# The opening of a fused convolution and max-out kernel: block 0's products put together, and work handed between engines

## The chip, the cores and the metric

The kernel runs on one core of a Trainium2 chip. A core has a matrix engine (TensorE, PE in the profile, with its weight loads as PEld), three engines that work element by element (VectorE or DVE, ScalarE or ACT, GpSimd or POOL) and a sequencer that issues the DMA transfers here (SyncE or SP). Each engine runs its own instructions in the order in which the program gives them, and waits on semaphores for the others. The metric is the device time of one execution, in microseconds (us).

## The reference: what is computed

```
w   = softmax(weight, axis=-1)                    # 8 heads x 7 taps
y   = causal convolution of x along the sequence  # x: 8 x 4160 x 192, 24 channels a head
      y[b, s, h, :] = sum_k w[h, k] * x[b, s + k - 6, h, :]
h   = max(y @ w1, y @ w2, y @ w3)                 # 33280 tokens, 192 -> 768
out = h @ w_out                                   # 768 -> 192
```

Inputs and output are float32.

## The kernel before, in words

The 33280 tokens are cut into 65 blocks of 512. The kernel uses max(a, b, c) = c + max(0, a - c, b - c). It forms the differences w1 - w3 and w2 - w3 once (`wd`, made by `make_wd`), computes max(0, y(w1 - w3), y(w2 - w3)) with one relu on ScalarE and one maximum on VectorE (`top`, L500 and L501), and adds y(w3 w_out) through a 192x192 matrix `m16` that it also makes once (`make_m`). The 768 columns of the weights are handled as 6 tiles of 128, and the opening speaks of thirds: tiles 0 to 1, 2 to 3 and 4 to 5.

All work runs in the order in which the program is written (the schedule is manual), so the order of the lines is the order on each engine.

Weights. `load_wa` brings channels 0 to 127 and `load_wb` channels 128 to 191 of w1, w2 and w3, in pieces of columns, all through the SP queue. For the last 64 channels, w1 lies in partitions 0 to 63 and w2 in 64 to 127 of one slot, so w3's 64 rows are needed in both halves: `copy_w3` (L314 to L316) copies them from the lower to the upper half. `make_wd(n, j0, j1)` (L312) subtracts for n = 0 (w1, channels 0 to 127), n = 1 (w2, the same channels) and n = 2 (channels 128 to 191 of both). `cast_w3` makes a 16-bit copy of w3, `cross_wd` (L323) swaps halves of `wd`.

The band. The convolution is done on TensorE as a product with a banded matrix of the softmax weights. L293 makes the band's 38 distinct columns for all heads by small matmuls into PSUM, in two tiles cut at column `CUT`; L297 copies them to the four diagonal places of `band`, the first tile on ScalarE, the second on VectorE. `keep_warm` (L261) issues matmuls on zeros.

Blocks 0 to 3 are "dense". `load_x` brings their rows as float32 (`xf`); `cast_dense` (L216) writes them as 16-bit into two zeroed arrays `xz[t][0]` and `xz[t][1]`, by slots of 32 channels; blocks 0 and 2 share one pair of arrays, 1 and 3 the other. `conv_dense` (L388) multiplies them with the band: its half n = 0 gives channels 0 to 127, its half n = 1 channels 128 to 191 in both halves of the partitions. Each half is 40 matmuls into its own PSUM tile `D`, copied (L393) by the engine that the call names to `yd[:, 0]` or `yd[:, 2]`. `cross` (L399) writes `yd[:, 1]`, the swapped halves of `yd[:, 0]`, for the blocks that need it (2 and 3). Later blocks have rows laid out differently; part of their `xf` (partitions 32 to 63) must be zeroed first (`zero_x`, L137 and L140) before `load_x` may bring them.

Products of blocks 0 and 1 (`l1_dense`, L536) are named by letters: F is the product over channels 0 to 127, H the one over channels 128 to 191, where both sides (w1 and w2) use half of TensorE's rows each and run side by side. The tiles named `lp` and `lq` live in the PSUM pools p and q, `lw` in pool w. For blocks 0 and 1 `l1_dense` and `tops` alternate, two tiles of 128 columns at a time. Block 0 runs F then H, block 1 H then F.

The opening, as written before (lines L687 to L712): differences of the first third on VectorE, conv of block 0 (copies on ScalarE and VectorE), loads of blocks 4 to 6, the casts of block 1, F of block 0's first two tiles, w3's later columns copied by GpSimd and most of the later differences there, conv of block 1 (half n = 1 first, copied by ScalarE; then n = 0, copied by VectorE), H of block 0's first two tiles, and then block 1's first two tiles, H then F.

Of the kernel before, what the change touches and what calls it, by code (L numbers as in the profile page):

```python
# [11 lines left out]
FP16 = mybir.dt.float16  # L12
# [3 lines left out]
P = 128  # L16
# [12 lines left out]
def kernel(  # L29
# [177 lines left out]
    def cast_dense(t, copies, slots_=range(CYC // 32)):  # L207
        xf, _, parts = xin.pop(t)
        for v, copy in enumerate(copies):
            if copy is None:  # L210
                continue
            for s in slots_:
                cut = GRP * (32 * s // GRP + 1)
                a, b = (32 * s, cut) if v == 0 else (cut, 32 * s + 32)
                for (rl, q0, q1) in parts:
                    copy(  # L216
                        out=xz[t][v][0:rl, q0:q1, :].rearrange("p q (k c) -> p q k c", c=CYC)[:, :, :, a:b],
                        in_=xf[0:rl, q0:q1, :].rearrange("p q (k c) -> p q k c", c=CYC)[:, :, :, a:b])
# [33 lines left out]
    make_identity(nc, ident[:])  # L252
    ident16 = const.tile([P, P], FP16)
    nc.gpsimd.tensor_copy(out=ident16[:], in_=ident[:])
    idle = const.tile([P, NBLK], FP16)
    nc.vector.memset(idle[:], 0.0)
    def keep_warm(n, pool=psw, tag="w"):

        ps = pool.tile([P, NBLK], FP32, tag=tag, name="idle")
        for _ in range(n):  # L260
            nc.tensor.matmul(ps[:], lhsT=idle[:, 0:P], rhs=idle[:], start=True, stop=True)  # L261

    line = const.tile([NHEAD, LINE // 2], FP16, name="line")[:, 0:WIN + 31]
    nc.vector.memset(line[:], 0.0)
    for v in range(2):
        nc.vector.memset(xz[0][v][:], 0.0)  # L270
# [5 lines left out]
    bands = const.tile([P, LINE // 2 * ceil(NHEAD * BAND_W * 2 / LINE)], FP16, name="band")  # L276
    band = bands[:, 0:NHEAD * BAND_W].rearrange("p (h w) -> p h w", w=BAND_W)
    nc.vector.memset(band[:], 0.0)
    keep_warm(5, psp, "p")
    wrec = const.tile([NHEAD, SMALL], FP32, name="wrec")[:, 0:1]  # L280
    nc.vector.reduce_sum(out=wrec[:], in_=wexp[:], axis=AXX)
    nc.vector.reciprocal(out=wrec[:], in_=wrec[:])
    zero_x(4)
    nc.vector.tensor_scalar_mul(out=line[:, 31:31 + KW], in0=wexp[:, 0:KW], scalar1=wrec[:])
    for v in range(2):
        nc.vector.memset(xz[1][v][:], 0.0)  # L286
    cast_dense(0, (nc.vector.tensor_copy, nc.vector.tensor_copy))
    CUT = 28
    for lo, hi, copy in ((0, CUT, nc.scalar.copy), (CUT, WIN, nc.vector.tensor_copy)):
        bps = psq.tile([32, hi - lo + 3, NHEAD], FP32, tag="q", name=f"band_{lo}")  # L290
        for c in range(lo, hi):

            nc.tensor.matmul(bps[:, c - lo:c - lo + 4, :].rearrange("p c h -> p (c h)"),  # L293
                             lhsT=line[:, WIN - 1 - c:WIN + 31 - c],
                             rhs=ident16[0:NHEAD, 0:4 * NHEAD], start=True, stop=True)
        for a in range(4):
            copy(out=band[32 * a:32 * a + 32, :, 32 * a + lo:32 * a + hi],  # L297
                 in_=bps[:, 0:hi - lo, :].rearrange("p c h -> p h c"))
    zero_x(5)
    keep_warm(3, psp, "p")  # L300

# [12 lines left out]
    def copy_w3(copy, j0, j1):  # L314
        f = slice(P * j0, P * j1)
        copy(out=w3s[HALF:P, 1, f], in_=w3s[0:HALF, 1, f])  # L316
# [59 lines left out]
    def conv_dense(t, copies, pools=((None, None),) * 2, order=(0, 1)):  # L376


        yd = dense[t] = ydp.tile([P, NC, NBLK], FP16, tag="yd", name=f"yd_{t}")
        for n in order:  # L380
            slots_ = ((0, 1, 2, 3), (4, 5, 4, 5))[n]
            pool, tag = pools[n]
            ps = (pool or psw).tile([P, NBLK], FP32, tag=tag or "w", name=f"D{n}_{t}")
            for (q, b, row_lo, rlen, lo, hi, cc) in chunks_of[t]:
                for v in range(2):
                    for g, s in enumerate(slots_):
                        h = (32 * s + 31 * v) // GRP
                        nc.tensor.matmul(  # L388
                            ps[32 * g:32 * g + 32, lo:hi],
                            lhsT=xz[t][v][0:rlen, q, 32 * s:32 * s + 32],  # L390
                            rhs=band[0:rlen, h, cc:cc + hi - lo],
                            start=(v == 0), stop=(v == 1), tile_position=(0, 32 * g))
            copies[n](out=yd[:, 2 * n, :], in_=ps[:])  # L393

    def cross(t, copy=nc.vector.tensor_copy):

        yd = dense[t]
        for i in range(2):
            copy(out=yd[HALF * i:HALF * (i + 1), 1, :], in_=yd[HALF * (1 - i):HALF * (2 - i), 0, :])  # L399

    def evac(t, i, copy=nc.scalar.copy):
# [138 lines left out]
    def tops(*tiles):  # L540
        for t, j in tiles:
            top(t, j, (open_ps[t, j, 0], open_ps[t, j, 1]))
# [143 lines left out]
    GP = nc.gpsimd.tensor_copy  # L686
    make_wd(0, 0, 2)  # L687
    make_wd(1, 0, 2)
    zero_x(6, 4, NR, nc.vector)
    conv_dense(0, (ACT, DVE))  # L690
    zero_x(6, 0, 4)
    for t in range(NDENSE, XBUF):
        load_x(t)
    copy_w3(DVE, 0, 2)
    make_wd(2, 0, 2)
    cast_dense(1, (GP, ACT), (1, 2, 0))
    l1_dense([(0, 0, PQ), (0, 1, PQ)], "F")
    cast_w3(0, 2)
    copy_w3(GP, 2, 6)
    make_wd(2, 2, 4, nc.gpsimd)  # L700
    for n in range(NC):
        make_wd(n, 4, 6, nc.gpsimd)
    cast_w3(2, 6)
    conv_dense(1, (DVE, ACT), order=(1, 0))
    make_wd(0, 2, 4)
    make_wd(1, 2, 4)
    cross_wd(0, GP)
    GP(out=wo[:], in_=wos[:])
    l1_dense([(0, 0, PQ), (0, 1, PQ)], "H")
    tops((0, 0), (0, 1))  # L710
    l1_dense([(1, 0, WW), (1, 1, WW)], "HF")
    tops((1, 0), (1, 1))  # L712
    l1_dense([(0, 2, PQ), (0, 3, PQ)], "FH")
# [10 lines left out]
    cross_wd(1, ACT)  # L724
    first_hidden(0)
    first_hidden(1)
    conv_dense(2, (ACT, ACT), (WW[0], PQ[1]))
    cast_x(4)
    cross(2)
    make_m(0)  # L730
    make_m(1)
    zero_x(0, NQ)
# [24 lines left out]
    for t in range(2, NB):  # L757
        u = convs_at.get(t, NB)
        late = t > 2 and u < NB
        if t in (3, 4):  # L760
            double(t + 1)
        if t > 3:
            for v in range(casts.get(t - 1, 8) + 1, casts[t] + 1):
                cast_x(v)
        l1(t, 0)
        if t == 2:
            first_rest()
        elif t == 3:
            cast_x(8)
            nc.gpsimd.tensor_copy(out=m16[0:HALF, 2, :], in_=m16[HALF:P, 0, :])  # L770
            nc.gpsimd.tensor_copy(out=m16[HALF:P, 2, :], in_=m16[HALF:P, 1, :])
        if t > 3 and not late:
            op(lambda t=t: (store(t - 2, 0, 4, (nc.sync,)),
                            turn(t + 2, (2,)) if place(t + 2)[1:] in ((0, 4), (0, 5)) else None,
                            turn(t + 1, (4,)) if place(t + 1)[1:] == (0, 5) else None, load_on(t)))
        else:
            op(lambda t=t: store(t - 2, 0, 4, (nc.sync,)))
        cuts = ROOM if late else EVEN
        st2(t - 1, (cuts[0], cuts[0]))
        for j in range(1, NJ):  # L780
            l1(t, j)
            if late and j == 1:
                st2(t - 1, (cuts[0] + OWN + AHEAD, cuts[0] + OWN))
                meet()
                quad, second = u >= QUADS, u < QUADS or t == u - 3
                conv(u, WPWQ, range(4 * second, 4 * second + 4) if quad else range(NHEAD))
                for i in (0, 2):
                    evac(u, i)
                for i in (1, 3):
                    evac(u, i, nc.vector.tensor_copy)  # L790
                if second:
                    turn(u)
                load_on(t)
            if t == 2 and j == 1:
                meet()
                conv_dense(3, (ACT, DVE))
                zero_x(1, NQ, NR, nc.vector)
                cross(3, GP)
                load_x(8)
                cast_x(6)  # L800
            elif t == 2 and j == 3:
                meet()
                conv(u, WW)
                evac(u, 0)
                evac(u, 1, nc.vector.tensor_copy)
                turn(4)
                load_x(9)
                cast_x(7)
            st2(t - 1, (cuts[j], cuts[j]))
            if j == 1 and t > 4 and t + 2 in pairs and pairs[t + 2][1] % 2 == 0:  # L810
                double(t + 2)
            if t == NB - 1 and j == 3:
                op(lambda: store(NB - 2, 0, 2, (nc.sync,)))
        if t == NB - 1:
            op(lambda: store(NB - 2, 2, 4, (nc.sync,)))
# [29 lines left out]
```

## Time and profile before

| what | value |
|---|---|
| median of 3 runs | 453.33 us (453.15 to 453.54) |
| the profiled execution's own time | 453.45 us |
| its span, from the first to the last instruction | 451.7 us |
| busy: TensorE, VectorE, ScalarE, GpSimd | 447.2, 357.0, 319.2, 203.8 us |
| conv of block 0 on TensorE | from 6.29 us, 1.91 us with its last matmul |
| conv of block 1 on TensorE | from 10.01 us, 1.52 us |
| H of block 0's first two tiles | from 11.47 us |
| block 1's first products | from 11.91 us |
| GpSimd's copy of w3's later columns | from 12.56 us, 0.86 us |

A line of a timeline reads: start, duration, engine, line of the program, operation, tile written and tiles read, shape written and read, count, and in brackets the idle time before it and what ended that. A line with a count above one merges neighbours, and its duration is that of all of them. The times of PE are those of pipelined instructions, so neighbours overlap; from start to start is the better measure.

### The profile page before, as it was taken

Reading aid. Unit: us, or ns where it says so; the run is one execution under the profiler, and the core shown is the slowest. Engines: PE = TensorE matmul, PEld = TensorE weight load, DVE = VectorE, ACT = ScalarE, POOL = GpSimd, SP = SyncE. Lnnn points to the kernel's source line nnn. Section 1 sums busy time; section 2 is a strip of 40 time slices with the busy share of each in tenths; the row PEclk is TensorE's granted clock in tenths of the full one; section 3 lists DMA queues with packets and bytes.
Section 4 is the critical chain, followed back from the end, with each engine's and each line's share of the span. In section 5 each row is a group of like instructions: output and inputs, shape, how many; then the busy total and the mean of one; then the engine's idle time right before and its main releaser. Section 6 shows DMA issues by size and latency. Waiting matters only on the chain.

```text
span 451.7 us, 18257 instructions
## 1 busy us (share of the span) xinstructions
PE 447.2 (99%) x7574; PEld 410.0 (91%) x7574; DVE 357.0 (79%) x610; ACT 319.2 (71%) x597; POOL 203.8 (45%) x234
## 2 busy tenths in 40 slices
PE   8999999999999999999999999999999999999997
PEld 4569999999999999999999999999999999999996
DVE  7778778878878788787787887887887887887775
ACT  7867777767777676676776776776776776776664
POOL 2865836556464534724824624626543645124000
PEclk9999999999999999999999999999999999999999
DMA  7969997596886759749649749759549656152123
GB/s 205 249 171 168 207 190 201 143 206 176 174 217 155 170 122 201 176 116 201 166 131 194 179 109 189 196 106 212 165 114 193 173 152 151 53 136 75 58 71 106
DMA packets 128242, 72.01 MB, mean 159 GB/s; under 512 B 52320, under 2 KB 127967, under 8 KB 128159
## 3 DMA queue, kind: packets, MB, share of 16 engines
q1 hardware_dynamic: 127999, 70.75, 68.8%
q8 instruction: 59, 0.97, 1.0%
q14 instruction: 24, 0.20, 0.2%
q10 hardware_dynamic: 160, 0.10, 0.1%
HBM read 33.28 MB, written 25.56 MB: 130 GB/s over the span
## 4 chain that ended last, share of the span: by engine, by line
PE 97%; DVE 1%; ACT 0%; issue 0%; ACTq 0%
PE po L577 36%; PE lq L513 32%; PE lp L513 22%; PE G L367 3%; PE lw L536 1%; PE lp L536 1%; PE D L388 1%; PE po L635 0%; PE po L608 0%; PE lq L536 0%; DVE yd L399 0%; DVE xz L216 0%; DVE xz L286 0%; ACT L239 0%; DVE wd L312 0%
## 5 line engine op out<-in xcount | busy, mean ns | idle before, releaser
L577 PE MATMUL po<-wo,h 64*128 64x192 f16 x3024 | 331.9, 243 | 0.0
L501 DVE TENSOR_TENSOR h<-r,lq 128x512 f16<-128x512 f16 x384 | 262.9, 685 | 84.5 <-ACT r L500 74.8
L500 ACT ACTIVATE r<-lp 128x512 f16<-128x512 f32 x384 | 229.0, 597 | 114.3 <-PE lp L513 102.9
L513 PE MATMUL lp<-yp,wd 64*128 64x512 f16 x1098 | 295.6, 376 | 0.0
L513 PE MATMUL lq<-yp,wd 64*128 64x512 f16 x1098 | 295.5, 376 | 0.0
L577 PEld LDWEIGHTS <-h 64*128 64x128 f16 x3024 | 242.9, 94 | 5.5 <-issue 4.1
L513 PEld LDWEIGHTS <-wd 64*128 64x128 f16 x2268 | 181.7, 94 | 15.0 <-issue 0.2
L199 POOL CAST x<-xf 103x768 f16<-103x768 f32 x122 | 97.2, 825 | 113.4 <-DMA xf<-in_x_dram 98.3
L577 PE MATMUL po<-m,yp 64*128 64x192 f16 x720 | 140.3, 243 | 0.0
L430 POOL COPY yp<-yp 64x1536 f16<-64x1536 f16 (+1 forms) x70 | 90.9, 1298 | 85.4 <-DMA yp<-ys 53.7
L585 DVE TENSOR_TENSOR o<-a,po 128x384 f32<-128x384 f32 x126 | 69.0, 548 | 0.0
L577 PEld LDWEIGHTS <-yp 64*128 64x128 f16 x720 | 66.3, 94 | 0.1
L584 ACT COPY a<-po 128x384 f32<-128x384 f32 x126 | 59.5, 472 | 0.0
L407 ACT CAST ys<-G 128x480 f16<-128x480 f32 (+1 forms) x53 | 25.4, 530 | 9.5 <-PE G L367 9.5
L407 DVE CAST ys<-G 128x480 f16<-128x480 f32 (+1 forms) x53 | 30.2, 610 | 0.0
L367 PE MATMUL G<-x,band 39*32 39x240 f16 (+3 forms) x1024 | 16.5, 242 | 0.0
L367 PEld LDWEIGHTS <-band 39*32 39x32 f16 x1024 | 10.2, 91 | 4.6 <-issue 4.1
L513 PE MATMUL lq<-yd,wd 64*128 64x512 f16 x36 | 9.9, 376 | 0.2 <-DVE yd L399 0.2
L513 PE MATMUL lp<-yd,wd 64*128 64x512 f16 x36 | 9.7, 376 | 0.0
L536 PEld LDWEIGHTS <-wd 128*128 128x128 f16 (+1 forms) x48 | 3.2, 98 | 5.7 <-issue 2.4
L216 POOL CAST xz<-xf 112x160 f16<-112x160 f32 (+2 forms) x15 | 4.2, 328 | 7.8 <-DMA xf<-in_x_dram 7.8
L388 PEld LDWEIGHTS <-xz 112*32 112x32 f16 x320 | 4.9, 111 | 2.4 <-POOL xz L216 1.0
(76 smaller groups left out, 99.8 us busy)
## 6 DMA issues: line engine op xcount, KB each, us to landing
xf<-in_x_dram SPq DMA_DIRECT2D x113, 234.0 KB
out_dram<-o SPq DMA_DIRECT2D x62, 384.0 KB
wall<-in_moe_w_dram SPq DMA_DIRECT2D x12, 128.0 KB
xf<-in_x_dram SPq DMA_DIRECT2D x7, 204.8 KB
xf<-in_x_dram SPq DMA_DIRECT2D x3, 420.0 KB
yp<-ys SPq DMA_TRANSPOSE x70
out_dram<-o SPq DMA_DIRECT2D x5, 192.0 KB
wos<-in_moe_w_out_dram SPq DMA_DIRECT2D x1, 576.0 KB
```

Of the source, the lines that this page charges most:

```text
L199: nc.gpsimd.tensor_copy(out=x16s[t0][0:K, :, :, u, r, :].rearrange("p h j c -> p j h c"), in_=xf[0:K, 4 * r:4 * r + 4, :].rearrange("p j ( ...
L367: nc.tensor.matmul(G[2 * (k // per) + i][TOK * j:TOK * (j + 1), k % per, :], lhsT=band[row, h, HALF * i + LAP:HALF * i + KR], rhs=x16s[t0] ...
L388: nc.tensor.matmul(ps[32 * g:32 * g + 32, lo:hi], lhsT=xz[t][v][0:rlen, q, 32 * s:32 * s + 32], rhs=band[0:rlen, h, cc:cc + hi - lo], star ...
L407: copy(out=slots[t][:, i % 2, :, :, GRP * h0:GRP * (h0 + per)].rearrange("p u r (h c) -> p h (u r) c", c=GRP), in_=G[i][:].rearrange("p h ...
L430: nc.gpsimd.tensor_copy(out=yp[HALF * i:HALF * (i + 1), 1, :, :, :, :].rearrange("p i u k n -> p (i u k n)"), in_=yp[HALF * (1 - i):HALF * ...
L500: nc.scalar.activation(out=r[:], in_=ps[0][:], func=AF.Relu)
L501: nc.vector.tensor_max(out=hs[t][:, j, :], in0=r[:], in1=ps[1][:])
L513: nc.tensor.matmul(ps[i][:], lhsT=w_of(i, c, j), rhs=y_all(t, i, c), start=(n == 0), stop=(n == NC - 1))
L536: nc.tensor.matmul(open_ps[t, j, i][:], lhsT=a, rhs=b, start=(t, j, i) not in begun, stop=(t, j, i) in begun)
L577: nc.tensor.matmul(ps[b0, i][:, s % 2, :], lhsT=a, rhs=b, start=first, stop=last)
L584: nc.scalar.copy(out=a[:], in_=ps[s - 1, 0][:])
L585: nc.vector.tensor_add(out=outs[t][:, s - 1:s + 1, :], in0=a[:], in1=ps[s - 1, 1][:])
```

## The change

Four things change, all in the opening. (1) The band's matmuls use all 128 rows (`line` is zero outside the 8 heads' rows), `CUT` is 24 instead of 28, and the band is copied in two passes: heads 0 to 5 of both tiles, then heads 6 and 7. The matmuls on zeros get other widths. (2) Zeroing `xz[1]`, the second half of block 0's cast, and zeroing block 5's and 6's rows go to GpSimd. (3) Block 0's F and H are issued as one ahead of block 1's conv, with the relu and maximum behind them; both halves of block 0's conv are copied by ScalarE; half of block 1's cast goes from ScalarE to VectorE; w3's later columns are copied by ScalarE instead of GpSimd; the differences of the second third that were on VectorE go to GpSimd. (4) Block 2's conv is copied, and its halves are crossed, by ScalarE and VectorE instead of one engine each.

```diff
+    for v in range(2):
+        nc.gpsimd.memset(xz[1][v][:], 0.0)
...
-    def keep_warm(n, pool=psw, tag="w"):
+    def keep_warm(widths, pool, tag):
...
-    line = const.tile([NHEAD, LINE // 2], FP16, name="line")[:, 0:WIN + 31]
+    line = const.tile([P, LINE // 2], FP16, name="line")[:, 0:WIN + 31]
...
-    keep_warm(5, psp, "p")
+    keep_warm((NBLK,) * 5 + (NBLK // 2, P // 2), psp, "p")
...
-    for v in range(2):
-        nc.vector.memset(xz[1][v][:], 0.0)
-    cast_dense(0, (nc.vector.tensor_copy, nc.vector.tensor_copy))
-    CUT = 28
+    cast_dense(0, (nc.vector.tensor_copy, nc.gpsimd.tensor_copy))
+    CUT = 24
...
-                             rhs=ident16[0:NHEAD, 0:4 * NHEAD], start=True, stop=True)
-        for a in range(4):
-            copy(out=band[32 * a:32 * a + 32, :, 32 * a + lo:32 * a + hi],
-                 in_=bps[:, 0:hi - lo, :].rearrange("p c h -> p h c"))
-    zero_x(5)
-    keep_warm(3, psp, "p")
+                             rhs=ident16[:, 0:4 * NHEAD], start=True, stop=True)
+        bands_.append((lo, hi, copy, bps))
+    keep_warm((NBLK, NBLK, NBLK // 2, P // 2), psp, "p")
+    for h0, h1 in ((0, 6), (6, NHEAD)):
+        for lo, hi, copy, bps in bands_:
+            for a in range(4):
+                copy(out=band[32 * a:32 * a + 32, h0:h1, 32 * a + lo:32 * a + hi],
+                     in_=bps[:, 0:hi - lo, h0:h1].rearrange("p c h -> p h c"))
+    zero_x(5, eng=nc.gpsimd)
+    zero_x(6, eng=nc.gpsimd)
...
-    zero_x(6, 4, NR, nc.vector)
-    conv_dense(0, (ACT, DVE))
-    zero_x(6, 0, 4)
+    conv_dense(0, (ACT, ACT))
...
-    cast_dense(1, (GP, ACT), (1, 2, 0))
-    l1_dense([(0, 0, PQ), (0, 1, PQ)], "F")
+    cast_dense(1, (GP, DVE), (1, 2, 0))
+    l1_dense([(0, 0, PQ), (0, 1, PQ)], "FH")
+    tops((0, 0), (0, 1))
+    copy_w3(ACT, 2, 6)
+    make_wd(0, 2, 4, nc.gpsimd)
+    make_wd(1, 2, 4, nc.gpsimd)
     cast_w3(0, 2)
-    copy_w3(GP, 2, 6)
     make_wd(2, 2, 4, nc.gpsimd)
...
     conv_dense(1, (DVE, ACT), order=(1, 0))
-    make_wd(0, 2, 4)
-    make_wd(1, 2, 4)
     cross_wd(0, GP)
     GP(out=wo[:], in_=wos[:])
-    l1_dense([(0, 0, PQ), (0, 1, PQ)], "H")
-    tops((0, 0), (0, 1))
     l1_dense([(1, 0, WW), (1, 1, WW)], "HF")
...
-    conv_dense(2, (ACT, ACT), (WW[0], PQ[1]))
+    conv_dense(2, (ACT, DVE), (WW[0], PQ[1]))
     cast_x(4)
-    cross(2)
+    cross(2, ACT, DVE)
...
-                cross(3, GP)
+                cross(3, GP, GP)
```

More of the change, by code (lines that the diff above doesn't have):

```diff
@@ L254 @@
     nc.gpsimd.tensor_copy(out=ident16[:], in_=ident[:])
+    for v in range(2):
+        nc.gpsimd.memset(xz[1][v][:], 0.0)
     idle = const.tile([P, NBLK], FP16)
     nc.vector.memset(idle[:], 0.0)
-    def keep_warm(n, pool=psw, tag="w"):
+    def keep_warm(widths, pool, tag):
         ps = pool.tile([P, NBLK], FP32, tag=tag, name="idle")
-        for _ in range(n):
-            nc.tensor.matmul(ps[:], lhsT=idle[:, 0:P], rhs=idle[:], start=True, stop=True)
-    line = const.tile([NHEAD, LINE // 2], FP16, name="line")[:, 0:WIN + 31]
+        for n in widths:
+            nc.tensor.matmul(ps[:, 0:n], lhsT=idle[:, 0:P], rhs=idle[:, 0:n], start=True, stop=True)
+    line = const.tile([P, LINE // 2], FP16, name="line")[:, 0:WIN + 31]
     nc.vector.memset(line[:], 0.0)
@@ L283 @@
     zero_x(4)
-    nc.vector.tensor_scalar_mul(out=line[:, 31:31 + KW], in0=wexp[:, 0:KW], scalar1=wrec[:])
-    for v in range(2):
-        nc.vector.memset(xz[1][v][:], 0.0)
-    cast_dense(0, (nc.vector.tensor_copy, nc.vector.tensor_copy))
-    CUT = 28
+    nc.vector.tensor_scalar_mul(out=line[0:NHEAD, 31:31 + KW], in0=wexp[:, 0:KW], scalar1=wrec[:])
+    cast_dense(0, (nc.vector.tensor_copy, nc.gpsimd.tensor_copy))
+    CUT = 24
+    bands_ = []
     for lo, hi, copy in ((0, CUT, nc.scalar.copy), (CUT, WIN, nc.vector.tensor_copy)):
@@ L393, in conv_dense, with cross @@
             copies[n](out=yd[:, 2 * n, :], in_=ps[:])
-    def cross(t, copy=nc.vector.tensor_copy):
+    def cross(t, *copies):
         yd = dense[t]
-        for i in range(2):
+        for i, copy in enumerate(copies):
             copy(out=yd[HALF * i:HALF * (i + 1), 1, :], in_=yd[HALF * (1 - i):HALF * (2 - i), 0, :])
```

## The prediction

> **What bounds the kernel now.** I read the page first, then the windows, then the timelines of the engines over the first 14 us. Times are microseconds from the start of the span.
>
> ```profile
> span 451.7 us, 18257 instructions
> PE 447.2 (99%) x7574; PEld 410.0 (91%) x7574; DVE 357.0 (79%) x610; ACT 319.2 (71%) x597; POOL 203.8 (45%) x234
> PE 97%; DVE 1%; ACT 0%; issue 0%; ACTq 0%
> ```
>
> TensorE is the bound: it is 97% of the chain that ended last. From 11.47 on I find only two matmul starts late by more than 0.11: 0.35 before L513 at 25.26 and 0.19 near 31.5. So a microsecond by which TensorE's stream is ahead or behind at about 12 us reaches the end of the span almost whole. What counts is the time at which TensorE begins block 1's first product. The TensorE timeline gives it: 11.91.
>
> ```profile
> 8.60 0.63 PE L536 MATMUL lq<-yd,wd 128*128 128x512 f16 x1
> 10.01 1.52 PE L388 MATMUL D<-band,xz 112*32 112x103 f16 x80
> 11.47 0.39 PE L536 MATMUL lp<-yd,wd 64*128 64x512 f16 x1
> 11.91 1.77 PE L536 MATMUL lw<-yd,wd 64*128 64x512 f16 x8
> 13.52 0.38 PE L536 MATMUL lp<-yd,wd 128*128 128x512 f16 x1
> ```
>
> Next the other engines around the same place: ScalarE, then GpSimd.
>
> ```profile
> 9.39 0.78 ACT L216 CAST xz<-xf 112x160 f16<-112x160 f32 x3 [0.37 <-DMA xf<-in_x_dram]
> 11.12 0.59 ACT L393 CAST yd<-D 128x512 f16<-128x512 f32 x1 [0.95 <-PE D L388]
> 11.89 1.08 ACT L500 ACTIVATE r<-lp 128x512 f16<-128x512 f32 x2 [0.18 <-PE lq L536]
> ...
> 9.44 1.02 POOL L216 CAST xz<-xf 112x160 f16<-112x160 f32 x3 [7.77 <-DMA xf<-in_x_dram]
> 12.56 0.86 POOL L316 COPY wall<-wall 64x512 f32<-64x512 f32 x1 [1.54 <-DMA wall<-in_moe_w_dram]
> 13.51 2.78 POOL L312 TENSOR_TENSOR wd<-wall 128x256 f16<-128x256 f32 x4
> ```
>
> The row to see is POOL L316. This copy of w3's later columns waits for a transfer whose last update the trace puts at 12.43, and nobody needs it soon. ScalarE meanwhile drains conv 1's first result at 11.12, which lets TensorE go on at 11.91.
>
> **The change part by part.**
>
> Front, up to conv 0. More idle matmuls (320 columns, 0.27 at 0.427 for 512) fill the hole from 3.34 to 3.72: no cost. The second idle group has 1344 columns instead of 1536: 4.84 + 1.12 = 5.96. VectorE loses two memsets (0.97) and half of six casts (0.5 of 1.00). But x's second part lands only at 4.50, so its three casts run 4.55 to 5.02 and three band copies of about 0.24 (row of 32x80: 0.23) end by 5.8. ScalarE's first four band copies (144 elements; 0.335 for 224, less 80 at 0.84 ns, 0.27) start at 4.57 and end by 5.7. So the idle matmuls let conv 0 start at about 6.05 instead of 6.29: gain 0.24. The band copies for heads 6 and 7 (four of 0.19 each on ScalarE and VectorE, until 6.8) are hidden behind conv 0's first half, 0.86 long until 6.91; uncovered they would cost up to 0.8. GpSimd's three casts (1.02 by the row above) end at 5.6, hidden by the idle matmuls. Its memsets of xz (two, about 0.5 each) and of xf (32x1536 twice; 0.25 for 192 elements and 0.20 for 128 make 1.2 to 1.5 each) lie in its 7.77 of idle time. SP's loads of blocks 5 and 6 wait for the latter, ready by 8.6, but are issued after 14.7: nothing.
>
> Block 0's products. Conv 0 ends near 7.8; ScalarE drains both halves (0.59 each) until 8.6; VectorE makes the differences by 7.6 and 8.4. First product 7.87 to 9.6, third product (row pairs, 2 x 0.427 at the slow rate) to 10.45. In the trace the third ran at 11.47 to 11.91, so 0.43 of work leaves the place after conv 1. Conv 1 needs GpSimd's casts (10.13 for its first half, 10.46 for the second, both behind the load that landed at 9.31), so it runs 10.5 to 11.55. Up to here TensorE is 0.35 ahead (11.91 against 11.55).
>
> The step that decides: the copy of w3 moves from GpSimd to ScalarE, ahead of conv 1's drain. ScalarE's order becomes: two drains of conv 0, two relus of block 0's tiles (done by about 11.6), the copy, conv 1's drain of the half that the third product reads, and with it all further relus. The transfer does not move: all loads before it on SP keep their order. So the copy starts at 12.43 + 0.08 (the wait after a landing in ScalarE's L216 row: 9.31 to 9.39). Its own time on ScalarE is not in the trace; 112x240 took 0.39, 64x768 took 0.83, and in between the slope gives 0.61. I keep 0.39 and 0.83 as ends. Then the drain, 0.59, and 0.06 to TensorE: 12.51 + 0.61 + 0.59 + 0.06 = 13.77. Block 1's products begin with the third ("HF"), so TensorE, in order, stands from 11.55 to 13.77; that the other half was long drained by VectorE does not help it. Against 11.91: **+1.86** (1.6 to 2.1 with the ends of the copy). The gains of the front are swallowed, since TensorE waits in any case.
>
> Behind it. GpSimd loses the copy (0.86) and gets two differences at 0.70 (2.78 for four), but starts them at 10.5, in the time that it now stands waiting: differences done at 12.7, the last third at 16.1, wo at 19.1, against need 1.86 later than now. Nothing. VectorE's differences cost 0.34 each; they leave an engine that is not waited for: nothing.
>
> Block 2. Draining on two engines and splitting the cross between them takes about 0.7 out of a chain that held TensorE for 0.35 (VectorE 23.44 to 25.20). But ScalarE's cross (0.61) now stands ahead of the copies of m, whose PSUM buffers the next product wants: that start slips by about 0.17, and the third product still waits 0.1 to 0.2. I take a gain of 0.05 (0 to 0.35). Block 3's cross names GpSimd twice, as now.
>
> Sum on the profiled execution of 453.45 (span 451.7 and 1.75 around it): +1.86 - 0.05 = 455.25. That execution is 0.12 above the median 453.33, so **455.1**.
>
> **The clock, an unknown beside it.** A change of TensorE's rate is seen at both ends of the trace. Matmuls of 512 columns start 0.427 apart until 10.76 and 0.213 afterwards. At the other end the granted clock halves at 451.08, though the last matmul began at 448.56:
>
> ```profile
> 10.76:14.17 3.41, 3.41 (x78) 1.69 (x67) 2.58 (x6) 2.76 (x5) 1.78 (x3) 1.00 0.91 255
> 447.67:451.08 3.41, 1.13 (x14) 0.90 (x11) 0.71 (x2) 0.64 (x2) 0.00 (x0) 1.00 0.52 173
> 451.08:451.70 0.62, 0.00 (x0) 0.00 (x0) 0.00 (x0) 0.00 (x0) 0.00 (x0) 0.50 0.00 0
> ```
>
> (Columns: stretch, length, busy time of PE, PEld, DVE, ACT and POOL, clock, DMA share, GB/s.) So 2.5 without a matmul, at the end of 3.4 with a third of them busy, was enough to halve the rate. The standstill to come, 2.2, is a little shorter, so I take no halving, and keep it as a rival. Its price: after a stop the slow rate would last as long as dense work took to lift it here, at least from 8.21 and at most from 6.29 to 10.76, 2.55 to 4.5, of which half is lost: 1.3 to 2.2. I take the middle, 1.7.
>
> The Trainium skill (TensorE: Matmul & The Clock Gate, "Why this matters for your kernels") asks only that there be no TensorE gap above about 3 us; by that rule 2.5 would not have halved the rate, which the row above contradicts. By the rule the sum stays at 455.1, by the row it is at 455.1 or 456.8. The page's window of 3.413 us (section "What's actually happening") fits the trace, in which 10.76 and 451.08 are 129.0 such windows apart.
>
> **The rivals.**
>
> B. The same standstill, and the rate halves: 455.1 + 1.7 = 456.8. For it: the row before 451.08. Against: 2.2 is less than 2.5, and products follow it.
>
> C. The transfer lands sooner. Of its 16 updates, 15 came by 11.21 and one at 12.43; an instruction fetch of 16 KB began at 9.18 and took 1.1. If no update is late, ScalarE is free at 11.3 at the earliest and, behind the relus, at 11.6 at the latest. TensorE goes on at 12.55 to 12.86, +0.64 to +0.95: 453.9 to 454.2. Against it: the fetch must run some time before this transfer ends, and what it delays is queued ahead of the transfer's last part.
>
> D. Not slower: w3's piece is there when ScalarE reaches the copy, and ScalarE gets there early because the rate doubles sooner. The matmuls that build the band now use 128 rows instead of 8, so TensorE might count as busy from 3.7 on, not from 6.29, and the rate double 2.6 sooner, near 8.2. Then block 0's products end at 9.4, its relus at 10.5, conv 1 at 11.1, the copy at 11.1; TensorE goes on at 11.8, 0.1 earlier. With block 2's gain of up to 0.35 that is 452.9 to 453.3. It decides from a landing before 10.7 (10.7 + 0.08 + 0.61 + 0.59 + 0.06 = 12.04, and 0.1 more makes it slower). Against: the first of the 16 updates came at 10.40, the last 1.7 after that point.
>
> **How the numbers follow.** About 0.2% (0.9 us) is what measuring this kernel can tell from no change. Chances: the forecast (A) 0.46, B 0.27, C 0.12, D 0.10, and 0.05 for a gain over 0.9 by a path that I do not see. A alone spans 454.7 to 455.5. The range leaves out D, the unseen gain and the tail of B: 453.8 to 456.9. A and B are slower by over 0.2%, and so is most of C (from 454.2 on): 0.82. D's better half and the unseen gain count 0.08 for faster, since D's 452.9 can fall past the bound with the spread of the runs; the rest, 0.10, lies within.
>
> **What the profile after would show.** Right: ScalarE's copy row (64x512) with over 0.5 of idle time released by the DMA of the weights, conv 1's drain right behind it, and on TensorE a gap of about 2 before block 1's products, at about 13.8; conv 0 from about 6.05. B: product starts 0.43 apart again after 14. Wrong: a copy that starts before 11.2; a landing well ahead of 12.43; a gap made good later, which needs TensorE waits after 14 that I don't see; or new waits for GpSimd's differences, which then would start after 13.

## The result, and the profile after

The changed kernel takes 456.46 us (median; 455.99 to 456.95, 4 runs), the kernel before 453.44 (453.15 to 453.71, 4 runs) beside it: ratio 1.0065, 95% interval 1.005 to 1.008. The change makes the kernel slower by about 3 us. The forecast was 455.1 with a range of 453.8 to 456.9. The sign and the main mechanism came as predicted. The time lies inside the range, but beside rival B (456.8) and not beside the forecast.

The profiled executions (456.81 after, 453.45 before) differ by 3.36. The page after, its span, its busy times and the first line of its chain of waits:

```profile
span 455.0 us, 18271 instructions
PE 447.4 (98%) x7577; PEld 410.0 (90%) x7577; DVE 354.8 (78%) x608; ACT 317.9 (70%) x598; POOL 209.9 (46%) x242
PE 96%; SPq 1%; DMA 1%; ACT 0%; issue 0%; DVE 0%
```

TensorE is still the bound, and its busy time has hardly moved (447.4 against 447.2). So the 3 us are not more work. They are time in which TensorE stood, or in which its matmuls took longer at half its rate. The second part hides in the busy time, because the rate also rose earlier here (at 5.40, the start of the first window below, against 10.76 before). TensorE's timeline after, around the place that the prediction named:

```profile
8.07 0.38 PE L541 MATMUL lq<-yd,wd 128*128 128x512 f16 x1
...
9.69 1.35 PE L393 MATMUL D<-band,xz 112*32 112x103 f16 x80 [0.30 <-POOL xz L216]
13.69 2.86 PE L541 MATMUL lw<-yd,wd 64*128 64x512 f16 x8 [2.65 <-ACT yd L398]
16.35 0.63 PE L541 MATMUL lp<-yd,wd 128*128 128x512 f16 x1
...
20.44 0.38 PE L541 MATMUL lp<-yd,wd 128*128 128x512 f16 x1
```

Two things are to be seen. Block 1's first product begins at 13.69 after 2.65 of idle time that ScalarE's drain ended. And the matmuls of 512 columns that took 0.38 at 8.07 take 0.63 at 16.35 (0.43 from start to start, against 0.21), and 0.38 again at 20.44. ScalarE and GpSimd after, in the same place:

```profile
9.21 1.09 ACT L505 ACTIVATE r<-lp 128x512 f16<-128x512 f32 x2 [1.25 <-PE lq L541]
12.42 0.62 ACT L321 COPY wall<-wall 64x512 f32<-64x512 f32 x1 [2.12 <-DMA wall<-in_moe_w_dram]
13.06 0.59 ACT L398 CAST yd<-D 128x512 f16<-128x512 f32 x1
11.45 1.41 POOL L317 TENSOR_TENSOR wd<-wall 128x256 f16<-128x256 f32 x2 [1.23 <-DMA wall<-in_moe_w_dram]
```

ScalarE had nothing to do for 2.12, then made the copy of w3, and only then drained conv 1's result, which had lain in PSUM since 11.04 (13.69 less 2.65) at the latest. The chain of waits from 8 to 20 us says it in four rows:

```profile
7.20 5.19 DMA wall<-in_moe_w_dram
...
12.42 0.62 ACT wall L321
...
13.06 0.59 ACT yd L398
...
13.69 2.86 PE lw L541 x8
```

The rate stands in the granted clock. Columns of the windows: stretch, length, busy time of PE, PEld, DVE, ACT and POOL with their instructions, clock, DMA share, GB/s. After:

```profile
5.40:8.82 3.42, 2.90 (x90) 1.48 (x90) 3.12 (x11) 2.22 (x8) 2.69 (x2) 1.00 0.80 224
8.82:12.23 3.41, 1.89 (x84) 1.20 (x85) 2.57 (x6) 1.09 (x2) 1.75 (x5) 1.00 0.94 263
12.23:15.64 3.41, 1.95 (x7) 0.55 (x7) 0.00 (x0) 1.53 (x3) 3.34 (x6) 0.50 0.86 236
15.64:19.06 3.42, 3.42 (x13) 0.92 (x13) 1.38 (x2) 1.09 (x3) 2.82 (x4) 0.50 1.01 236
```

The clock halves at 12.23, in the middle of the standstill, and is whole again at 19.06: two stretches of 3.41.

Where the 3.36 are, by TensorE's position against before:

| place | before | after | difference |
|---|---|---|---|
| conv of block 0 starts | 6.29 | 5.79 | -0.50 |
| conv of block 1 starts | 10.01 | 9.69 | -0.32 |
| block 1's first product | 11.91 | 13.69 | +1.78 |
| conv of block 2 starts | 22.12 | 25.99 | +3.87 |
| conv of block 3 starts | 27.33 | 30.70 | +3.38 |
| last matmul starts | 448.56 | 451.93 | +3.37 |

So +1.78 at the standstill, +2.09 more by block 2 and 0.49 made good in block 2. The 2.09 belong to the halved rate: the work that before did from 11.91 to 14.95 (3.04) took 13.69 to 19.02 (5.33) after, which is +2.29; a further 0.20 comes back from there to block 2's conv.

### The profile page after: what moved, and what is told of

Read it like the earlier page. It is cut to its first block, busy times and chain, and to the rows that moved or that the text cites. A ratio compares the mean times of both kernels' runs of the same rounds, so it can differ in the third digit from the quotient of the medians.

```text
span 455.0 us, 18271 instructions
## 1 busy us (share of the span) xinstructions
PE 447.4 (98%) x7577; PEld 410.0 (90%) x7577; DVE 354.8 (78%) x608; ACT 317.9 (70%) x598; POOL 209.9 (46%) x242
## 4 chain that ended last, share of the span: by engine, by line
PE 96%; SPq 1%; DMA 1%; ACT 0%; issue 0%; DVE 0%
PE po L582 36%; PE lq L518 31%; PE lp L518 22%; PE G L372 3%; PE lw L541 1%; DMA wall<-in_moe_w_dram 1%; PE lp L541 1%; SPq L229 1%; PE D L393 0%; PE po L640 0%; PE po L613 0%; SPq L233 0%; SPq L167 0%; PE lq L541 0%; PE pm L352 0%
## 5 line engine op out<-in xcount | busy, mean ns | idle before, releaser
L372 PE MATMUL G<-x,band 39*32 39x240 f16 (+3 forms) x1024 | 16.5, 242 | 0.0
L372 PEld LDWEIGHTS <-band 39*32 39x32 f16 x1024 | 10.2, 91 | 4.6 <-issue 4.1
L541 PE MATMUL lw<-yd,wd 64*128 64x512 f16 (+1 forms) x24 | 6.0, 460 | 2.7 <-ACT yd L398 2.7
L506 DVE TENSOR_TENSOR h<-r,lw 128x512 f16<-128x512 f16 x6 | 3.9, 682 | 4.3 <-ACT r L505 4.3
```

The costliest lines, as they stand in the source:

```text
L372: nc.tensor.matmul(G[2 * (k // per) + i][TOK * j:TOK * (j + 1), k % per, :], lhsT=band[row, h, HALF * i + LAP:HALF * i + KR], rhs=x16s[t0] ...
L506: nc.vector.tensor_max(out=hs[t][:, j, :], in0=r[:], in1=ps[1][:])
L541: nc.tensor.matmul(open_ps[t, j, i][:], lhsT=a, rhs=b, start=(t, j, i) not in begun, stop=(t, j, i) in begun)
```

## The experiments

The theory: the copy of w3 on ScalarE, ahead of conv 1's drain, waits for a late transfer and holds the drain; the standstill that follows costs about 1.8 directly and lets the rate fall, which costs about 2 more. The rivals: the copy is harmless and something else of the change costs the time (the differences on GpSimd, block 2, the front); or the standstill alone costs it, and the slow matmuls are an accident of one execution. In what follows "conv 1" is the conv of block 1, and gains and losses of positions are those of TensorE.

### The copy behind the drain

All of the change is kept. On ScalarE the drain of conv 1 comes ahead of the copy.

```diff
     tops((0, 0), (0, 1))
-    copy_w3(ACT, 2, 6)
     make_wd(0, 2, 4, nc.gpsimd)
     make_wd(1, 2, 4, nc.gpsimd)
     cast_w3(0, 2)
+    conv_dense(1, (DVE, ACT), order=(1, 0))
+    copy_w3(ACT, 2, 6)
     make_wd(2, 2, 4, nc.gpsimd)
...
-    conv_dense(1, (DVE, ACT), order=(1, 0))
     cross_wd(0, GP)
```

> The changed kernel with one difference: on ScalarE, the copy of w3's later columns stands behind block 1's conv drain instead of ahead of it. Theory (the queue position on ScalarE makes the standstill, and the standstill makes the rate halve): block 1's first product starts near 11.0 instead of 13.69, no idle time of 2.7 on TensorE, the granted clock does not fall in the opening; the time is about 1.78 + 2.09 + up to 0.9 lower than the changed kernel's 456.5, that is 451.9 to 452.8, below the kernel before. Rival (the loss comes from the other reorderings, for instance the later differences on GpSimd or the products being put together): a wait of similar size for GpSimd's differences or for the weights takes its place, and the time stays above 454.5.

452.96 (452.83 to 454.39, 12 runs; before beside it 453.56, 35 runs): ratio 0.9988, interval 0.9973 to 1.0003. The timelines of TensorE and ScalarE:

```profile
11.19 1.93 PE L541 MATMUL lw<-yd,wd 64*128 64x512 f16 x8 [0.22 <-ACT yd L398]
...
10.55 0.59 ACT L398 CAST yd<-D 128x512 f16<-128x512 f32 x1 [0.43 <-PE D L393]
...
11.87 0.62 ACT L321 COPY wall<-wall 64x512 f32<-64x512 f32 x1 [0.73 <-DMA wall<-in_moe_w_dram]
```

The copy still waits for its transfer, until 11.87, and nothing minds: block 1's first product begins at 11.19, 0.72 earlier than before the change, and the clock does not fall. This one order costs the changed kernel 3.5 us (456.46 less 452.96). The result lies just above the expected 451.9 to 452.8, since TensorE has a new wait of 0.67 ahead of its product at 20.18, for `wo`, whose transfer landed near 18.9 (15.77 before the change). The gain over the kernel before is not established: the interval includes 1.

### The copy on GpSimd

```diff
-    copy_w3(ACT, 2, 6)
     make_wd(0, 2, 4, nc.gpsimd)
     make_wd(1, 2, 4, nc.gpsimd)
+    copy_w3(GP, 2, 6)
```

> The changed kernel with the copy of w3's later columns back on GpSimd, behind the two differences of the second third. Theory: no standstill before block 1's first product (start near 11.0), but GpSimd's copy (0.86) and then its difference (0.7) come later, so block 0's second pair of tiles waits for the difference until about 14.4: TensorE loses some 0.5 to 0.9 there. Time 452.4 to 453.4. Rival (reorderings at fault, not the copy's place): above 454.5.

454.43 (453.73 to 454.99, 10 runs): ratio 1.0015 (0.9998 to 1.0032). Above the expected range. The standstill is gone (block 1's first product at 11.05) and the clock does not fall, but two waits took its place, as TensorE's waits show (microseconds in total, times, longest):

```profile
PE lp L541 <- POOL wd L317: 1.2, 1, 1.2
PE lq L518 <- DVE yd L404: 1.0, 1, 1.0
```

The first is the last third's difference, which the copy on GpSimd pushed back. The second, at 25.20, is the cross of block 2, which should have been better off than before. VectorE and GpSimd there:

```profile
24.45 2.10 DVE L404 COPY yd<-yd 64x512 f16<-64x512 f16 x1
...
23.26 3.15 POOL L199 CAST x<-xf 103x768 f16<-103x768 f32 x4
```

The same instruction took 0.29 in the changed kernel. Here it ran inside GpSimd's casts and took 2.10. What follows: where the standstill goes, so does the fall; and GpSimd's work stretches VectorE's copies, which is taken up below.

### The kernel before with the copy on ScalarE

The rival that the copy is harmless is met from the other side: one line of the kernel before.

```diff
-    copy_w3(GP, 2, 6)
+    copy_w3(ACT, 2, 6)
```

> The kernel before with one difference: the copy of w3's later columns on ScalarE at the place where GpSimd had it, which is ahead of block 1's conv drain. Theory: the drain moves from 11.12 to about 13.1, block 0's third product from 11.47 to about 13.75, a standstill of some 2.3; plus 2.3 alone is 455.7, with a halved clock behind it up to 457.8. Rival (the copy on ScalarE is harmless by itself, and harm comes only together with the other parts): 453.2 to 453.8.

454.37 (453.8 to 456.56, 10 runs): ratio 1.0023 (1.0005 to 1.0041). The line alone makes the kernel slower, but by less than expected. Its profiled execution (455.78) shows the mechanism, in ScalarE's and TensorE's timelines:

```profile
12.30 0.62 ACT L316 COPY wall<-wall 64x512 f32<-64x512 f32 x1 [2.45 <-DMA wall<-in_moe_w_dram]
12.94 0.59 ACT L393 CAST yd<-D 128x512 f16<-128x512 f32 x1
...
13.57 1.82 PE L536 MATMUL lw<-yd,wd 64*128 64x512 f16 x8 [2.25 <-ACT yd L393]
```

The first product is 1.66 late here; the clock halves at 14.78 for one stretch, the lateness grows to 2.85 by block 2's conv, and 0.55 is made good there, leaving 2.30. The ten runs fall into two groups: six of 453.8 to 454.5 with a mean clock of 0.999 or 1.0, and four of 455.8 to 456.6 with 0.996. So the rate falls in some executions of this kernel and not in others, and those in which it falls take about 1.8 longer (the middles of the groups, 455.9 and 454.1). In the profiled one, 1.19 of that came between the first product and block 2's conv (2.85 less 1.66); how late the first product was in the others is not recorded, so the rest is not explained.

### The standstill filled

The changed kernel with 12 idle matmuls of 512 columns where TensorE stands:

```diff
+    keep_warm((NBLK,) * 12, psp, "p")
     l1_dense([(1, 0, WW), (1, 1, WW)], "HF")
```

> The changed kernel with 12 matmuls on zeros (512 columns each, 2.56 us at the fast rate) on TensorE between block 1's conv and block 1's products, so that TensorE waits as long as before but is not idle. Theory (half rate follows from the idle stretch): block 1's first product still starts at about 13.7, the granted clock stays at 1.0 from its first rise on, and the time falls by about 2.1 against the changed kernel, to 454.2 to 454.6: what remains is the wait alone, 1.78 less the 0.49 that block 2's part brings. Rival (the rate falls for another reason, for instance because an early rise does not last, or because of the small gaps between 8.3 and 9.7): the clock falls in the opening all the same and the time stays at 455.9 to 457.

455.05 (454.59 to 455.51, 10 runs): ratio 1.0025 (1.001 to 1.004). TensorE's timeline:

```profile
11.05 2.76 PE L263 MATMUL idle<-idle 128*128 128x512 f16 x12
13.84 1.58 PE L541 MATMUL lw<-yd,wd 64*128 64x512 f16 x8
15.25 0.38 PE L541 MATMUL lp<-yd,wd 128*128 128x512 f16 x1
```

Block 1's first product starts as late as in the changed kernel (13.84 against 13.69), but the matmuls behind it run at the full rate, and the mean clock is 1.0 in all ten runs. Up to block 2's conv this gives 2.27 back, against 2.1 expected. By the medians only 1.41 is left (0.86 against the changed kernel's repeat, below), so the expected 454.2 to 454.6 was missed: 0.69 is lost again in a wait at 32.66 for which the profile names no releaser. The two costs are thereby parted: the delay and the rate.

### The changed kernel again

The same file once more, to see whether its fall of the rate is an accident.

> The changed kernel itself again, on the same chip as the others. Theory (a standstill of 1.8 always, and a halved rate that lasts one or two windows of 3.4 or does not come, depending on where the windows fall): times in groups, about 455.0 without a fall, 456.0 with one window and 456.9 with two; the median between 455.5 and 457. Rival (the fall of the rate is tied to the program's start and always the same): all times within 0.5 of each other.

455.91 (455.75, 455.77, 456.06 and 456.91): ratio 1.0061 (1.0039 to 1.0084). No execution was without a fall. Of the eight executions in all, five had a mean clock near 0.996 (one stretch at half rate; 455.75 to 456.1) and three 0.992 (two stretches; 456.81 to 456.95). The profiled execution here had one. TensorE's timeline, and the window before the fall at 13.71:

```profile
13.38 2.57 PE L541 MATMUL lw<-yd,wd 64*128 64x512 f16 x8 [1.95 <-ACT yd L398]
```

```profile
10.30:13.71 3.41, 1.43 (x83) 1.15 (x83) 1.88 (x4) 1.20 (x2) 2.77 (x5) 1.00 0.77 206
```

So the fall belongs to this kernel, and how many stretches it lasts differs by execution. The kernel before has it too, but seldom: 2 of its 93 executions timed beside the experiments have a mean clock of 0.996, and they are the slowest (456.44 and 457.18).

### The band on 8 rows

Rival D of the prediction rested on the band's matmuls counting as busy when they use 128 rows. The kernel with the copy behind the drain gets the 8 rows of before.

```diff
-    line = const.tile([P, LINE // 2], FP16, name="line")[:, 0:WIN + 31]
+    line = const.tile([NHEAD, LINE // 2], FP16, name="line")[:, 0:WIN + 31]
...
-                             rhs=ident16[:, 0:4 * NHEAD], start=True, stop=True)
+                             rhs=ident16[0:NHEAD, 0:4 * NHEAD], start=True, stop=True)
```

> The kernel of the run with the copy behind the drain, with one difference: the matmuls that build the band use 8 rows, as in the kernel before, not 128. In the traces so far the fast rate came at 4.1 to 6.0 us with 128 rows (four traces) and at 7.95 and 10.76 with 8 rows (two traces). Theory (matmuls on few rows do not count as work for the rise of the rate): it rises between 7.3 and 10.8 here; block 0's products run at the slow rate for most of their 1.3 us of fast work and block 1's conv starts up to 0.9 later; time 453.0 to 453.8 against 452.96. Rival (the rise depends on the idle matmuls' widths or on chance): it rises by 6.5 as with 128 rows, and the time stays at 452.7 to 453.2.

453.67 (452.96 to 455.32, 10 runs): ratio 1.0008 (0.9996 to 1.002), inside the expected range and 0.7 above its parent's 452.96. TensorE's timeline:

```profile
9.19 0.63 PE L541 MATMUL lq<-yd,wd 128*128 128x512 f16 x1
10.72 1.16 PE L393 MATMUL D<-band,xz 112*32 112x103 f16 x80
```

Block 0's products still take 0.63 each. The full rate comes between 10.2 and 10.8, at 5.99 in the parent. The 0.7 can't be put down to the rate alone: this trace also has a wait of 0.64 ahead of 28.90, in block 3's conv, for which the profile names no releaser.

### The kernel before with the band on 128 rows

The counterpart, with the shape of the band's matmuls alone:

```diff
-    line = const.tile([NHEAD, LINE // 2], FP16, name="line")[:, 0:WIN + 31]
+    line = const.tile([P, LINE // 2], FP16, name="line")[:, 0:WIN + 31]
...
-                             rhs=ident16[0:NHEAD, 0:4 * NHEAD], start=True, stop=True)
+                             rhs=ident16[:, 0:4 * NHEAD], start=True, stop=True)
```

> The kernel before with one difference: the band's matmuls use all 128 rows (the new rows hold zeros in one operand). If few rows are what kept the rate from rising, it rises between 4.1 and 7.0 here instead of 7.9 to 10.8, block 0's F takes 0.9 instead of 1.7, but block 1's conv still waits for its casts until about 10.1, so only its own 0.4 and up to 0.2 more are gained: 0.2 to 0.6 below the kernel before. If rows don't matter, no change of the rise and the time within 0.2 of the kernel before.

452.97 (452.27 to 455.06, 12 runs) against 453.45: ratio 0.9993 (0.9979 to 1.0006). The size is as expected, but the interval includes 1. The trace is plain about the rate, in the window that ends where it rises, and in a product of block 0 behind it:

```profile
3.37:6.79 3.42, 3.23 (x70) 1.91 (x73) 3.21 (x15) 3.21 (x6) 0.00 (x0) 1.00 0.68 188
```

```profile
8.45 0.38 PE L536 MATMUL lq<-yd,wd 128*128 128x512 f16 x1
```

The kernel before had a window of the same length with TensorE busy throughout, and it did not lift the rate; the band's matmuls, of 8 rows, lie in it:

```profile
3.93:7.35 3.42, 3.42 (x92) 2.21 (x92) 3.22 (x14) 3.22 (x6) 0.00 (x0) 1.00 0.72 172
```

### Block 2, as before and on GpSimd

Two runs ask whether block 2 should be changed at all, with the copy behind the drain kept. The first puts block 2 back:

```diff
-    conv_dense(2, (ACT, DVE), (WW[0], PQ[1]))
+    conv_dense(2, (ACT, ACT), (WW[0], PQ[1]))
...
-    cross(2, ACT, DVE)
+    cross(2, DVE, DVE)
```

> The kernel of the run with the copy behind the drain, with the block 2 part undone: both drains of block 2's conv on ScalarE, both crosses on VectorE. The changed kernel made good 0.49 at this place. Theory (the gain came from GpSimd standing idle at that moment, since VectorE's cross took 0.29 there and 0.80 to 2.10 where GpSimd was casting): the time changes by less than 0.3, to 452.8 to 453.3; VectorE's two crosses take about 0.3 to 0.6 each where GpSimd is idle. Rival (the gain came from splitting the work over two engines): TensorE waits 0.35 or more again before the third product and the time rises by 0.4 to 0.6, to 453.4 to 453.6.

The second leaves VectorE out of the cross:

```diff
+    cross(2, ACT, GP)
     cast_x(4)
-    cross(2, ACT, DVE)
```

> The kernel of the run with the copy behind the drain, with VectorE's half of block 2's cross on GpSimd instead, and that ahead of GpSimd's casts of block 4. A copy of 64x512 takes GpSimd 0.64. If VectorE and GpSimd slow each other here, the order on one engine takes that away: the cross ends about 24.8 on the scale of that run, TensorE waits less than 0.2 before the third product, and the time is 452.6 to 453.0 with a smaller spread. If block 4's casts, now 0.7 later, are needed on time, a new TensorE wait appears near 28 to 31 us and the time is above 453.2.

Block 2 as before: 452.71 (452.33 to 455.4, 12 runs), ratio 0.9993 (0.9978 to 1.0007). The cross on GpSimd: 453.67 (452.34 to 454.22, 12 runs), ratio 0.9995 (0.9982 to 1.0008). The first keeps no wait at block 2; its two crosses and GpSimd's casts:

```profile
22.88 0.61 DVE L404 COPY yd<-yd 64x512 f16<-64x512 f16 x2 [2.38 <-ACT yd L398]
...
23.37 1.60 POOL L199 CAST x<-xf 103x768 f16<-103x768 f32 x2 [0.35 <-DMA xf<-in_x_dram]
```

The crosses start 0.5 ahead of the casts and take 0.30 each; in the kernel before the change the casts started 0.96 ahead of them and they took 0.88 each on average. The second removes the wait for the cross too, but its median missed the expected 452.6 to 453.0: the trace loses 0.65 at 31.78, again with no releaser named, and 0.31 at 27.19. A time above 453.2 was expected only if block 4's casts came late, but the matmuls that read them (L372, from 30.07) did not wait. Neither differs from the kernel before by a measurable amount.

The first was run again, to see whether 452.71 holds:

> The kernel of the run with block 2 as before, unchanged, a second time, to tell whether it is faster than the kernel before: 452.5 to 452.9 again, 0.5 to 0.9 below the kernel before, or within 0.3 of it if the first time was luck.

453.49 (452.49 to 454.66, 12 runs), ratio 0.9995 (0.9977 to 1.0013): it does not. One execution had a mean clock of 0.996, the profiled one (454.23). There block 1's rows landed late, and conv 1 waited; the window ahead of the fall at 11.82:

```profile
10.35 1.35 PE L393 MATMUL D<-band,xz 112*32 112x103 f16 x80 [1.23 <-POOL xz L216]
```

```profile
8.40:11.82 3.42, 1.95 (x85) 1.24 (x85) 2.00 (x7) 1.63 (x3) 1.50 (x4) 1.00 0.87 248
```

The longest gap here is the 1.23 of the row above, and the rate still fell.

### The differences on VectorE

To the kernel with block 2 as before, this one gives the two differences of the second third back to VectorE, behind its drain of conv 1.

```diff
-    make_wd(0, 2, 4, nc.gpsimd)
-    make_wd(1, 2, 4, nc.gpsimd)
...
     conv_dense(1, (DVE, ACT), order=(1, 0))
+    make_wd(0, 2, 4)
+    make_wd(1, 2, 4)
     copy_w3(ACT, 2, 6)
```

> The kernel of the run with block 2 as before, and the two differences of the second third back on VectorE, behind its drain of block 1's conv. VectorE stood idle there, from 11.7 to 13.1; GpSimd's chain gets 1.4 shorter, and block 0's second pair, which waited 0.26 for GpSimd's third difference, can start its H when w1's and w2's last rows have landed, near 13.2. Time 452.2 to 452.8, no more than 0.3 below that run's 452.71, if TensorE's other waits stay as they are; if GpSimd's casts of block 4, now earlier, meet VectorE's crosses, those take 0.8 or more each, TensorE waits there again and the time is 453.0 or above.

453.92 (453.1 to 455.35, 12 runs), ratio 1.0013 (1.0001 to 1.0025): missed, and slower at the edge of what can be told. VectorE's and TensorE's timelines of its profiled execution:

```profile
8.95 1.61 DVE L216 CAST xz<-xf 112x160 f16<-112x160 f32 x3 [0.30 <-DMA xf<-in_x_dram]
...
12.41 1.34 PE L541 MATMUL lw<-yd,wd 64*128 64x512 f16 x5 [0.46 <-DVE yd L398]
```

VectorE's casts of block 1 took 1.61, against 0.72 in the other variants. GpSimd cast beside them there too, so what made them longer here is open. Conv 1 stood after five matmuls until 10.09, and block 1's F waited 0.46 for VectorE's drain. A wait of 0.85 at 27.48 has no releaser. Nothing here speaks for VectorE as the place of these differences.

## Why the prediction was right or wrong

**The decisive step was right.** "The copy of w3 moves from GpSimd to ScalarE, ahead of conv 1's drain" gave +1.86 and measured +1.78. Its terms: the transfer landed at 12.39 (12.43 predicted), the copy started at 12.42 (12.51), took 0.62 (0.61, between ends of 0.39 and 0.83), the drain took 0.59, block 1's first product began at 13.69 (13.77). The copy behind the drain shows it by undoing it, the kernel before with one line changed by doing it alone.

**The step that failed is the clock: "so I take no halving".** Two errors lie in it. The standstill was put at 2.2 and was 2.65 by its row. The rate rose at 5.40, so block 0's F and H ended at 9.4 instead of 10.45 and conv 1 at 11.04 instead of 11.55; what TensorE gained in front of a fixed landing only lengthened the gap. And the comparison was of the wrong kind: it set the length of one gap (2.2) against another (2.5), but in these traces the busy share of a whole window of 3.41 separates the falls from the rest. The window ahead of the fall held 1.89 of work, and in the last run of block 2 as before 1.95 was little enough with no gap above 1.23. The price of the halving was put at 1.7 (1.3 to 2.2) and measured 2.09 over two stretches; executions with one stretch end about 0.9 lower (455.75 to 456.1 against 456.81 to 456.95). With the halving the sum is rival B, 456.8; the median is 456.46. The stated range held the result because it had kept B in, not because the forecast's own case (454.7 to 455.5) came. That B lies so near is in part luck: the halving cost 0.39 more than its price and block 2 gave back 0.44 more than its term (below), and the two nearly cancel.

**The front.** Conv 0 started at 5.79, not 6.05, since the idle matmuls' last ones ran at the doubled rate, and it then stood for 0.15 on the band's copies, which the prediction had hidden. The steps named as swallowed were swallowed: TensorE was 0.50 ahead at conv 0, 0.32 ahead at conv 1, and none of it lasted.

**GpSimd** was right in its result: differences 0.70 each, done at 12.86 (12.7). They started at 11.45 and not at 10.5, since they waited 1.23 for a transfer of weights that the prediction had not counted. After them come the last third, done at about 16.25 (16.1), and `wo` at 19.80 (19.1; 0.54 went into waiting for its transfer). In the changed kernel TensorE waits for none of them.

**Block 2 was mis-sized.** A gain of 0.05 (0 to 0.35) was taken; 0.49 came. The prediction priced VectorE's cross as in the kernel before, while its size depends on what GpSimd does. Block 2's conv arrived 3.87 later, and VectorE's cross then found GpSimd's casts just over. The timelines of GpSimd, ScalarE and VectorE after:

```profile
24.55 3.28 POOL L199 CAST x<-xf 103x768 f16<-103x768 f32 x4 [0.90 <-DMA xf<-in_x_dram]
27.30 0.62 ACT L404 COPY yd<-yd 64x512 f16<-64x512 f16 x1
27.87 0.29 DVE L404 COPY yd<-yd 64x512 f16<-64x512 f16 x1
```

GpSimd and VectorE before:

```profile
22.48 1.60 POOL L199 CAST x<-xf 103x768 f16<-103x768 f32 x2
23.44 1.76 DVE L399 COPY yd<-yd 64x512 f16<-64x512 f16 x2 [2.37 <-ACT yd L393]
24.23 1.66 POOL L199 CAST x<-xf 103x768 f16<-103x768 f32 x2 [0.15 <-DMA xf<-in_x_dram]
```

VectorE copied at 0.29 once GpSimd had finished (24.55 + 3.28 = 27.83), and at 0.88 on average beside it. The kernel before with the copy on ScalarE made good 0.55 there without any change to block 2; its two crosses took 1.09 together, against 1.76. So the gain comes at least in part from being late, and not from handing the drain and the cross to two engines; block 2 as before shows no loss without that part.

**The rivals.** B was right on the mechanism and near in size. C did not happen: in the nine traces where ScalarE waited for this transfer, the copy started between 11.86 and 12.56. D's premise held, the 128 rows do let the rate rise sooner, but its condition, a landing before 10.7, was missed by 1.7, and the early rise made the standstill longer instead.

## What to carry to other kernels

Before an instruction is moved to another engine, ask what it waits for there and what is queued behind it: a copy that waited harmlessly on GpSimd held a drain, and with it the bounding engine, once it stood ahead of that drain on ScalarE; the same copy one place further back cost nothing. Price a standstill of TensorE by the busy share of the windows around it as well, since half of the loss here came after the gap was over. And when work is pulled ahead of a wait whose end is fixed, it lengthens the gap and gains nothing.

## What the runs showed of the hardware that was not expected

**The rate of TensorE.** Events of one execution lie a multiple of 3.41 apart, at another phase in each execution. The rate fell behind windows with TensorE busy for 1.13 (end of the kernel before), 1.21 (the kernel before with the copy on ScalarE), 1.43, 1.89 and 1.95 of 3.41. It did not fall behind windows with 2.12 (the ends of the copy behind the drain and of the cross on GpSimd) and more. At half rate, a window with 1.95 did not lift it (after, 12.23 to 15.64). These runs leave the bound open between 1.95 and 2.12. The length of a gap alone does not tell: with the copy on GpSimd TensorE stood for 1.21 between two windows with 2.81 and 2.67 busy, and the rate held; 1.23 went with a fall in the window with 1.95. The window of the kernel before with the copy on ScalarE, behind which the rate fell:

```profile
11.37:14.78 3.41, 1.21 (x8) 0.42 (x8) 1.56 (x5) 2.43 (x5) 1.41 (x2) 1.00 0.89 265
```

A window of the copy behind the drain, and what follows it, where the rate held:

```profile
446.31:449.72 3.41, 2.12 (x26) 1.90 (x23) 1.32 (x4) 0.64 (x2) 0.00 (x0) 1.00 0.43 145
449.72:451.30 1.58, 0.00 (x0) 0.00 (x0) 0.00 (x0) 0.00 (x0) 0.00 (x0) 1.00 0.18 61
```

The Trainium skill (TensorE: Matmul & The Clock Gate, "Why this matters for your kernels") asks for no gap above about 3 us. Neither the 2.65 after nor the fall without a gap above 1.23 fits it; the measurement decides, and by it shorter gaps count when they share a window.

**Rows of a matmul.** With the band's matmuls on 128 rows the rate rose at 4.1 to 6.9 in nine traces, with 8 rows at 7.95, 10.2 to 10.8, and 10.76 in three. In the kernel before, the window from 3.93 to 7.35 was busy throughout, about 0.9 of it with matmuls on 8 rows, and did not lift it. Where the windows lie is not the reason: one from 1.13 to 4.54 with 3.12 busy, 0.8 of it on 8 rows (the kernel before with the copy on ScalarE), did not lift the rate, and one from 0.89 to 4.30 with 3.07 busy (block 2 as before, 128 rows) did.

**VectorE beside GpSimd.** The copy of 64x512 in 16 bits took 0.29 with GpSimd idle, 0.88 on average beside casts in the kernel before, and 2.10 inside them with the copy on GpSimd. There it ended at 26.55, 0.14 after the last cast (23.26 + 3.15 = 26.41); with the standstill filled, 0.42 long from 25.60, it ended 0.14 after casts that ended at 25.88. The traces hold 18 such copies by VectorE in block 2's cross. The ten that took longer than 0.29 all began while GpSimd was in an instruction and ended 0.14 after the end of one; the eight of 0.29 began with GpSimd idle or at most 0.15 before the end of its instruction. So it looks as if the copy waits until GpSimd's instruction is over. The Trainium skill (Advanced Engine Details and Errata, "VectorE Performance Modes") says that VectorE's second port to SBUF is shared with GpSimd, so that GpSimd's instructions and those of VectorE that use both ports can hold each other up; the rows agree with it. That the port is the cause was not tested by itself.

**What stays open.** Waits of TensorE of 0.5 to 0.85 between 27.5 and 33.4, for which the profile names no releaser, stand in four traces (the standstill filled, the band on 8 rows, the cross on GpSimd, the differences on VectorE); their cause was not found, and they are as large as what separates the better variants. No variant was shown to beat the kernel before: the copy behind the drain (0.9988), block 2 as before (0.9993 and 0.9995) and the 128 rows alone (0.9993) all have intervals that include 1.
